# Attention and expert routing on one core: where a batch's gating stands in the turns of the attention loop

## The chip, the cores and the metric

The kernel runs on one core of one Trainium2 chip. The metric is the device time of one execution in microseconds (us); lower is better. Before the change the median of three runs is 442.36 us (441.19, 442.36 and 442.59).

The engines in the rows: PE is TensorE's matmuls, PEld its weight loads, DVE is VectorE, ACT is ScalarE, POOL is GpSimd, SP is SyncE, which here issues most of the DMAs. Each engine works through its own instructions in the order in which they were written for it, and waits where an operand or a buffer isn't there yet.

## The reference, cut to what matters

Blocked causal attention for 8 batches of 8 heads, 576 tokens of 64 values each, with blocks of 64; its output, 4608 tokens of 512 values, goes into a mixture of 8 experts in which each token has one expert and each expert keeps the 80 tokens with the largest gate weight:

```python
scores = where(block_i >= block_j, q @ k.T / 8, -1e9)
attn = exp(scores - scores.max(-1)); attn /= attn.sum(-1)
x = (attn @ v)                       # [4608, 512]
logits = x @ w_gate                  # [4608, 8]
expert_idx = argmax(logits, 1)
gate_w = softmax(logits)[expert_idx]
for e in range(8):
    tok = the (at most) 80 tokens of expert e with the largest gate_w
    out[tok] = gate_w[tok] * (relu(x[tok] @ w1[e]) @ w2[e])   # all other rows 0
```

The gating is the part from logits to gate_w. The change concerns how and when it is done, batch by batch, while the attention of later batches goes on.

## The kernel before, in words

The attention works on 32 pairs of heads, four pairs to a batch. One pass of the loop `for i in range(-3, n + 2)` is called a turn here. The tuple TURN at the top of the file is a turn written out by hand: a list of operations, each with an offset that says which pair it belongs to. It fixes the order of the instructions on every engine. For one pair the operations are:

- `prep` (L409, DVE transpose, and L412, POOL) lays out q and k.
- `scores` (L427, with a mask product at L434) makes the scores of query rows in three groups, "3", "20" and "1"; `scores_4` (L443) makes those of the last 64 rows of both heads. Their results lie in PSUM tiles named sc, of which there are two. So "1" takes over the tile of "3", and `scores_4` that of "20".
- `max` (L448) and `max_4` (L452) take row maxima on DVE; `soft` (L456) and `soft_4` (L461) take the exponentials on ACT, each with a second instruction that reads the row sum.
- `back` (L492, and L475 for its small part "44") transposes the exponentials on PE in 64-row halves, in parts C, A and B. C needs `soft_4` of the turn before. `take` copies results out of PSUM, on ACT (L532) or DVE (L534).
- `values` 0 and 1 (L522) multiply by v; `flip` (L275) transposes the result on DVE for the store.

The PSUM tiles of `back`, `values` and the gating come from one pool of four, named pm.

Within a turn PE's order is: scores 3, back C, scores 20, [first step], back 44, values 0, scores 1, back A, values 1, scores_4, back B, [second step], [third step]. The three entries "step" of TURN each take one entry from a list `todo` and run it. DVE's order around them is: max 3, max 20, [first step], prep 1, max 1, copy of A, flip, max_4, copy of B, [second step], [third step], prep 0 of the next turn, max 3 of the next turn. ACT's is: copies of C, soft 3 twice, [first step], soft 0, soft 2, copy of 44, soft 2, soft 0, copy of values 0, soft 1 twice, copy of values 1, copy of A, [second step], soft_4, copy of B, [third step].

When a batch's four pairs are done, nine gating steps are put on `todo`: `recip` (L268 to L271, reciprocals of the row sums, DVE), `store` (six DMAs on SP), `logits` for the first 384 tokens and then for the other 192 (L292 on PE with a copy on ACT at L294), `logits2` for four token tiles and then for the fifth (L304 transposes on PE with all 128 rows, products with the reciprocals on DVE at L310, a sum over heads at L319), `gate` (nine DVE instructions from L327 to L341, and one exponential on ACT at L330), `turn` (L349, POOL) and `turn2` (L358, the placing product on PE, and its copy to Wt on DVE, L362). Three go into each of three turns; in every fourth turn the list is empty. The last batch's gating comes after the loop, written out in order, and there `logits2` is split at three tiles.

After the attention the candidates of each expert are ranked, the 80 tokens of each are gathered, and the two expert products run while weights are loaded.

Of the kernel before, what the change touches and what calls it, by code (L numbers as in the profile page):

```python
# [7 lines left out]
F32 = mybir.dt.float32  # L8
# [5 lines left out]
ALU = mybir.AluOpType  # L14
AX = mybir.AxisListType
# [3 lines left out]
P = 128  # L19
BLK = 64  # L20
NT = 5
# [57 lines left out]
def tile_attn_moe(ctx, tc, q, k, v, w_gate, w1, w2, capacity, out, xs=None, dbg=None):  # L79
    nc = tc.nc  # L80
    B, H, S, D = q.shape
    NTOK, DM = out.shape
    E, _, F = w1.shape
    NP = H // 2
# [7 lines left out]
    def tok0(t):  # L92
        return P * t

    def tokn(t):
        return BLK if t == NT - 1 else P
# [62 lines left out]
    prod = sm1.tile([P, NT, H, E], F32, name="prod")  # L159

# [22 lines left out]
    def constants():  # L183
# [7 lines left out]
        nc.gpsimd.memset(prod[:, NT - 1], 0.0)  # L191
# [64 lines left out]
    class Batch:  # L256
# [28 lines left out]
        def logits(self, half):  # L285

            q0, q1 = ((0, 384), (384, 576))[half]
            if half == 0:
                self.lgT = sm.tile([P, S], F32, name="lgT", bufs=1)
            lt = ps_m.tile([P, 512], F32, name="pm")  # L290
            for pr in range(NP):
                nc.tensor.matmul(lt[32 * pr:32 * pr + 32, 0:q1 - q0], lhsT=wgd[:, pr, :],  # L292
                                 rhs=self.xT[:, pr, q0:q1], start=True, stop=True, tile_position=(0, 32 * pr))
            nc.scalar.copy(self.lgT[:, q0:q1], lt[:, 0:q1 - q0])  # L294

        def logits2(self, half, ends=(4, NT)):
            la = ps_m.tile([P, 512], F32, name="pm")
            rs = self.rs
            if half == 0:
                self.lg = sm.tile([P, NT, E], F32, name="lg", bufs=2)  # L300
            t0, t1 = (0, *ends)[half:half + 2]
            for t in range(t0, t1):
                n = tokn(t)
                self.turned = nc.tensor.transpose(la[0:n, P * (t - t0):P * (t - t0 + 1)],  # L304
                                                  self.lgT[:, tok0(t):tok0(t) + n], ident)
            for u0, u1, n in ((t0, min(t1, NT - 1), P), (NT - 1, t1, BLK)):
                if u0 < u1:
                    nu = u1 - u0
                    iv = la[0:n, P * (u0 - t0):P * (u1 - t0)].rearrange("p (r c) -> p r c", r=nu * NP)[:, :, 0:2 * E]
                    nc.vector.tensor_tensor(  # L310
                        prod[0:n, u0:u1].rearrange("p t (r s) e -> p (t r) s e", s=2),
                        iv.rearrange("p r (s e) -> p r s e", s=2),
                        rs[0:n, u0:u1].rearrange("p t (r s) -> p (t r) s", s=2).unsqueeze(3)
                        .broadcast_to([n, nu * NP, 2, E]), op=ALU.mult)
            if half == 0 and ends[0] == NT - 1:
                return
            if ends[0] == NT - 1:
                t0 = 0
            nc.vector.tensor_reduce(self.lg[:, t0:t1], prod[:, t0:t1].rearrange("p t h e -> p t e h"), axis=AX.X,  # L319
                                    op=ALU.add)  # L320
# [238 lines left out]
    def step():  # L559
        if todo:  # L560
            f, *args = todo.pop(0)
            f(*args)

    with tc.manual_schedule():
        warm(WARM[0], ps_m.tile([P, 512], F32, name="pm"))
        for i in range(-3, n + 2):
# [22 lines left out]
            if i >= 2 and (i - 2) % NP == NP - 1 and i - 2 < n - 1:  # L589
                bt = batches[(i - 2) // NP]  # L590
                todo += [(bt.recip,), (bt.store,), (bt.logits, 0), (bt.logits, 1), (bt.logits2, 0), (bt.logits2, 1), (bt.gate,),
                         (bt.turn, nc.gpsimd)] + [(bt.turn2,)]
# [8 lines left out]
        bt.logits(0)  # L601
        bt.logits(1)
        bt.logits2(0, (3, NT))
        bt.logits2(1, (3, NT))
# [504 lines left out]
```

## Time and profile before

| | us |
|---|---|
| median of three runs | 442.36 |
| the profiled execution's own time | 441.93 |
| its span (first to last instruction) | 440.2 |

So 1.73 us of the profiled execution lie outside its span. In a timeline row the first number is the start from the beginning of the span, the second the time from the first start to the last end of the instructions that the row merges; then engine, line, operation, result and operands, shapes and the count. A bracket gives how long the engine sat idle before the row and what ended that. A matmul of two fp32 operands shows as two records. PE pulls weight loads ahead, and matmuls overlap, so the distance between two starts is what a step costs PE, not the duration in its row.

### The profile page before, as it was taken

The page shows a single profiled execution, that of the slowest core. Times are in us where ns is not written, and L with a number is a line of the kernel's source. Part 1 is how long each engine was busy: PE and PEld are TensorE (multiplying, and loading weights), DVE is VectorE, ACT ScalarE, POOL GpSimd, SP SyncE. Part 2 cuts the span into 40 slices and gives each one's busy share as a digit, 9 for nine tenths or more (in the row PEclk, how much of TensorE's full clock was granted, in tenths as well). Part 3 has the DMA queues.
Part 4 walks back from the last instruction along what each step waited for, and adds up shares of the span by engine and source line. Part 5 has one row for each costly group of instructions (what it writes and reads, how often), then busy time and mean ns, then how long its engine had stood idle before and what let it go on. Part 6 is the DMA issues. An engine that isn't in the chain of part 4 may idle for free. (4 is left out here: it accounts for less than half of the span.)

```text
span 440.2 us, 14257 instructions
## 1 busy us (share of the span) xinstructions
PE 409.2 (93%) x5755; PEld 263.4 (60%) x5755; DVE 280.1 (64%) x559; ACT 288.3 (65%) x887; POOL 65.9 (15%) x133
## 2 busy tenths in 40 slices
PE   5899999999999999999999999999868899999970
PEld 3466666666666566666666656666546855666510
DVE  5677788888798888879879887986682131100000
ACT  1698888798788879888887887888520123333230
POOL 5001111011111101112111010210026201100000
PEclk9899999999999999999999999999997899999996
DMA  9677878988786998898879887854087999999000
GB/s 130 117 133 165 174 125 212 241 171 165 190 164 130 158 291 171 167 210 178 170 136 281 167 173 192 179 128 110 2 224 245 324 405 410 412 401 357 20 15 21
DMA packets 230168, 84.34 MB, mean 192 GB/s; under 512 B 196877, under 2 KB 215309, under 8 KB 230096
## 3 DMA queue, kind: packets, MB, share of 16 engines
q1 hardware_dynamic: 222528, 64.91, 63.5%
q0 software_dynamic: 5200, 18.16, 11.9%
q8 instruction: 47, 0.77, 0.7%
q10 hardware_dynamic: 2368, 0.30, 0.6%
q14 instruction: 25, 0.20, 0.1%
HBM read 63.21 MB, written 20.33 MB: 190 GB/s over the span
## 5 line engine op out<-in xcount | busy, mean ns | idle before, releaser
L456 ACT ACTIVATE P<-sc,negm 128x128 f32<-128x128 f32 (+3 forms) x256 | 133.4, 531 | 16.2 <-DVE negm L448 14.5
L448 DVE TENSOR_REDUCE negm<-sc 128x2 f32<-128x1024 f32 (+3 forms) x128 | 100.6, 811 | 38.5 <-PE sc L434 38.4
L427 PE MATMUL sc<-T,T 64*128 64x128 f32 (+3 forms) x512 | 94.6, 468 | 2.2 <-POOL T L412 1.3
L492 PEld LDWEIGHTS pm<-ident,P 64*128 64x128 f32 x1536 | 56.4, 139 | 33.1 <-ACT xT L532 11.0
L492 PE MATMUL pm<-ident,P 64*128 64x64 f32 x1536 | 68.8, 229 | 1.9 <-DVE prod L310 0.4
L522 PE MATMUL pm<-PT,vn 128*64 128x128 f32 (+1 forms) x512 | 60.7, 379 | 0.0
L427 PEld LDWEIGHTS sc<-T,T 64*128 64x128 f32 x512 | 42.6, 191 | 23.7 <-issue 7.2
L412 POOL TENSOR_SCALAR T<-T 128x576 f32<-128x576 f32 x32 | 21.4, 668 | 227.0 <-DVE T L409 227.0
L456 ACT ACTIVATION_READ_ACCUMULATOR P<-sc,negm 128x1 f32 x256 | 52.6, 205 | 0.0
L409 DVE STREAM_TRANSPOSE T<-ld 128x576 f32<-128x576 f32 x64 | 48.7, 763 | 1.4 <-DMA ld<-in_q_dram 1.4
L522 PE MATMUL pm<-PF,vn 128*64 128x64 f32 (+1 forms) x768 | 48.2, 247 | 0.9 <-ACT PF L532 0.9
L522 PEld LDWEIGHTS pm<-PT,vn 128*64 128x64 f32 x512 | 33.5, 137 | 22.9 <-issue 22.9
L884 PE MATMUL av<-w,hT 128*32 128x512 f32 (+1 forms) x320 | 43.1, 594 | 1.6 <-DVE y L889 1.6
L532 ACT COPY PF<-pm 128x512 f32<-128x512 f32 x64 | 34.4, 588 | 15.0 <-PE pm L492 15.0
L843 PE MATMUL ps<-xsT,w 128*64 128x80 f32 x1024 | 40.7, 239 | 3.7 <-issue 3.7
L534 DVE COPY PT<-pm 128x512 f32<-128x512 f32 x64 | 43.5, 680 | 0.3 <-PE pm L492 0.3
L843 PEld LDWEIGHTS ps<-xsT,w 128*64 128x64 f32 x1024 | 38.3, 141 | 7.5 <-issue 7.0
L889 DVE SCALAR_TENSOR_TENSOR y<-av,comb,yt 80x512 f32<-80x512 f32 x8 | 6.0, 746 | 57.2 <-ACT yt L887 51.0
L443 PE MATMUL sc<-T,T 64*64 64x288 f32 x256 | 39.0, 424 | 1.2 <-ACT P L456 1.2
L461 ACT ACTIVATE P<-sc,negm 128x576 f32<-128x576 f32 x32 | 23.7, 741 | 22.1 <-DVE negm L452 22.1
L532 ACT COPY PT<-pm 128x512 f32<-128x512 f32 x64 | 37.8, 591 | 0.0
L522 PEld LDWEIGHTS pm<-PF,vn 128*64 128x64 f32 x768 | 32.0, 137 | 7.4 <-ACT PF L532 1.1
(168 smaller groups left out, 419.2 us busy)
## 6 DMA issues: line engine op xcount, KB each, us to landing
w<-in_moe_w_dram SPq DMA_DIRECT2D x13, 2048.0 KB, 19.2
ld<-in_q_dram SPq DMA_DIRECT2D x128, 72.0 KB, 3.2
out_dram<-zero POOLq DMA_DIRECT2D x18, 512.0 KB, 3.8
xs<-Y SPq DMA_DIRECT2D x32, 288.0 KB, 4.9
ld<-in_k_dram SPq DMA_DIRECT2D x124, 72.0 KB, 2.8
vn<-in_v_dram SPq DMA_DIRECT2D x64, 128.0 KB, 3.0
w<-in_moe_w_dram POOLq DMA_DIRECT2D x3, 2048.0 KB, 11.1
vt<-in_v_dram SPq DMA_DIRECT2D x32, 32.0 KB, 2.9
```

Source lines behind the costliest of these rows:

```text
L409: nc.vector.transpose(t, self.nat[x].rearrange("p g d -> p (g d)"))
L427: nc.tensor.matmul(s[:, h, c:c + P * (u + 1)], lhsT=self.T[0][r, P * u:P * (u + 1)], rhs=self.T[1][r, 0:P * (u + 1)], start=(x == 0), stop ...
L443: nc.tensor.matmul(s[r, c, 0:288], lhsT=self.T[0][r, 512:S], rhs=self.T[1][r, 288 * c:288 * (c + 1)], start=True, stop=True)
L448: nc.vector.tensor_reduce(self.negm[:, u], self.s[g][:, :, c:c + P * (u + 1)], axis=AX.X, op=ALU.max, negate=True)
L456: nc.scalar.activation(Pt[self.i % 2][u][:, h], self.s[g][:, h, c:c + P * (u + 1)], AF.Exp, bias=self.negm[:, u, h:h + 1], scale=1.0, accu ...
L461: nc.scalar.activation(Pt[self.i % 2][4][:, 0:S].rearrange("p (c k) -> p c k", c=2), self.s["4"][:, :, 0:288], AF.Exp, bias=self.negm[:, 4 ...
L492: nc.tensor.transpose(pt[c][:, n_ * BLK:(n_ + 1) * BLK], from_[r, P * j:P * (j + 1)], ident[r, r])
L522: nc.tensor.matmul(to, lhsT=lhs, rhs=rhs, start=(n_ == 0), stop=(n_ == len(steps) - 1))
L532: nc.scalar.copy(*self.out.pop((what, x)))
L534: nc.vector.tensor_copy(*self.out.pop((what, x)))
L843: yield nc.tensor.matmul(dst(b)[64 * c:64 * (c + 1)], lhsT=w_[:, a, col:col + 64], rhs=x_[:, a], start=(a == 0), stop=(a == n - 1))
L884: last = nc.tensor.matmul(to[col:col + s1 - s0], lhsT=hT[:, a, s0:s1], rhs=w_[:, a], start=(a == ends[0]), stop=(a == ends[1]), tile_posit ...
```

## The change

`logits` makes both products, of 384 and of 192 tokens, in one step, each with its own pm tile and copy. Its result lgT becomes one tile of 640 columns whose last 64 are zeroed once at the start (before, the product tile's last part was zeroed). `logits2` is one step: five token tiles are transposed in the two halves of 64 rows, ten transposes of 64 rows each into two pm tiles, then four products on DVE (one for each pair of heads, over all five token tiles) and one sum. An entry of `todo` may be None, which leaves a step empty. The list of a batch is now ten long: in its first turn logits, recip, store; in the second logits2, nothing, gate; in the third nothing, turn, nothing; in the fourth turn2.

```diff
+    lgT = sm1.tile([P, NT * P], F32, name="lgT")
...
-        nc.gpsimd.memset(prod[:, NT - 1], 0.0)
+        nc.gpsimd.memset(lgT[:, S:], 0.0)
...
+        def logits(self):
+
+            for q0, q1 in ((0, 384), (384, S)):
+                lt = ps_m.tile([P, 512], F32, name="pm")
+                for pr in range(NP):
+                    nc.tensor.matmul(lt[32 * pr:32 * pr + 32, 0:q1 - q0], lhsT=wgd[:, pr, :],
+                                     rhs=self.xT[:, pr, q0:q1], start=True, stop=True, tile_position=(0, 32 * pr))
+                nc.scalar.copy(lgT[:, q0:q1], lt[:, 0:q1 - q0])
+
+        def logits2(self):
+            la = [ps_m.tile([P, 512], F32, name="pm") for _ in range(2)]
+            self.lg = sm.tile([P, NT, E], F32, name="lg", bufs=2)
+            for t in range(NT):
+                for c in range(2):
+                    r = slice(c * BLK, (c + 1) * BLK)
+                    self.turned = nc.tensor.transpose(la[c][:, BLK * t:BLK * (t + 1)], lgT[r, P * t:P * (t + 1)],
+                                                      ident[r, r])
             for pr in range(NP):
...
+                iv = la[pr // 2][:, 0:BLK * NT].rearrange("p (t r c) -> p t r c", t=NT, r=2)[:, :, pr % 2, 0:2 * E]
+                nc.vector.tensor_tensor(
+                    prod[:, :, 2 * pr:2 * pr + 2], iv.rearrange("p t (s e) -> p t s e", s=2),
+                    self.rs[:, :, 2 * pr:2 * pr + 2].unsqueeze(3).broadcast_to([P, NT, 2, E]), op=ALU.mult)
+            nc.vector.tensor_reduce(self.lg, prod.rearrange("p t h e -> p t e h"), axis=AX.X, op=ALU.add)
...
     def step():
-        if todo:
-            f, *args = todo.pop(0)
-            f(*args)
+        x = todo.pop(0) if todo else None
+        if x:
+            x[0](*x[1:])
...
-                todo += [(bt.recip,), (bt.store,), (bt.logits, 0), (bt.logits, 1), (bt.logits2, 0), (bt.logits2, 1), (bt.gate,),
-                         (bt.turn, nc.gpsimd)] + [(bt.turn2,)]
+                todo += [(bt.logits,), (bt.recip,), (bt.store,), (bt.logits2,), None, (bt.gate,),
+                         None, (bt.turn, nc.gpsimd), None, (bt.turn2,)]
...
-        bt.logits(0)
-        bt.logits(1)
-        bt.logits2(0, (3, NT))
-        bt.logits2(1, (3, NT))
+        bt.logits()
+        bt.logits2()
```

## Rows read from the trace of the kernel before

**Rows 1.** The page: busy time of each engine and its share of the span.

```profile
PE 409.2 (93%) x5755; PEld 263.4 (60%) x5755; DVE 280.1 (64%) x559; ACT 288.3 (65%) x887; POOL 65.9 (15%) x133
```

**Rows 2.** Single turns, each from one start of scores 3 to the next: the stretch and its length, then busy time (and instructions) of PE, PEld, DVE, ACT and POOL, the granted clock of TensorE, the DMA share and GB/s. First a turn without gating, ahead of the first batch's gating; then the second, third and fourth turn of the first batch's gating; then the first turn of the second batch's.

```profile
54.49:63.50 9.01, 8.87 (x129) 5.74 (x127) 7.09 (x11) 7.84 (x25) 0.66 (x1) 1.00 0.69 124
73.40:83.38 9.98, 9.98 (x141) 6.52 (x137) 7.12 (x11) 8.27 (x28) 1.53 (x3) 1.00 0.99 298
83.38:92.61 9.23, 9.23 (x140) 6.15 (x139) 8.99 (x22) 7.68 (x26) 2.00 (x3) 1.00 0.81 150
92.61:101.38 8.77, 8.77 (x132) 5.80 (x125) 6.96 (x12) 7.84 (x25) 0.66 (x1) 1.00 0.90 153
101.38:111.28 9.90, 9.76 (x138) 5.94 (x134) 8.75 (x17) 8.37 (x26) 1.26 (x2) 1.00 0.81 175
```

**Rows 3.** The timeline of PE in the turn without gating: scores 3, back C, scores 1, scores_4 and back B (the next scores 3 starts at 63.50).

```profile
54.49 1.08 PE L427 MATMUL sc<-T,T 64*128 64x512 f32 x4
...
55.73 0.71 PE L492 MATMUL pm<-ident,P 64*128 64x64 f32 x16
...
59.92 0.70 PE L427 MATMUL sc<-T,T 64*128 64x256 f32 x4
...
61.84 1.19 PE L443 MATMUL sc<-T,T 64*64 64x288 f32 x8
62.95 0.72 PE L492 MATMUL pm<-ident,P 64*128 64x64 f32 x16
```

**Rows 4.** The timelines of ACT (soft_4 of the turn before, the two soft 3, then this turn's soft_4) and of DVE (max 3, and max 1 with the wait ahead of it) over the same turn.

```profile
54.85 0.74 ACT L461 ACTIVATE P<-sc,negm 128x576 f32<-128x576 f32 x1 [0.78 <-DVE negm L452]
...
57.44 0.70 ACT L456 ACTIVATE P<-sc,negm 128x512 f32<-128x512 f32 x1
...
58.11 0.70 ACT L456 ACTIVATE P<-sc,negm 128x512 f32<-128x512 f32 x1
...
63.87 0.74 ACT L461 ACTIVATE P<-sc,negm 128x576 f32<-128x576 f32 x1 [0.78 <-DVE negm L452]
...
56.02 1.18 DVE L448 TENSOR_REDUCE negm<-sc 128x2 f32<-128x1024 f32 x1
...
60.69 0.69 DVE L448 TENSOR_REDUCE negm<-sc 128x2 f32<-128x512 f32 x1 [1.25 <-PE sc L434]
```

**Rows 5.** The timeline of PE where gating stands: the product of 192 tokens and back 44 behind it; the five full transposes (scores 3 follows at 83.38) and back C of that turn; turn2 (scores 3 follows at 92.61); the product of 384 tokens (scores 3 follows at 111.28).

```profile
75.99 0.53 PE L292 MATMUL pm<-xT,wgd 128*32 128x192 f32 x8
76.45 0.30 PE L475 MATMUL pm<-ident,P 128*64 128x128 f32 x1
...
82.68 0.77 PE L304 MATMUL pm<-ident,lgT 128*128 128x128 f32 x5
...
84.37 0.70 PE L492 MATMUL pm<-ident,P 64*128 64x64 f32 x16
...
92.33 0.35 PE L358 MATMUL pm<-sp,sameR 128*32 128x40 f32 x16
...
110.49 0.85 PE L292 MATMUL pm<-xT,wgd 128*32 128x384 f32 x8
```

**Rows 6.** The weight loads of `back`: the page's group (busy us and mean ns of one), and the sixteen of one back B in the timeline of the weight loads.

```profile
L492 PEld LDWEIGHTS pm<-ident,P 64*128 64x128 f32 x1536 | 56.4, 139 | 33.1 <-ACT xT L532 11.0
...
53.94 0.57 PEld L492 LDWEIGHTS pm<-ident,P 64*128 64x128 f32 x16 [0.44 <-ACT xT L532]
```

**Rows 7.** The timeline of DVE around the start of the turn at 83.38: the two products and the sum of logits2, prep 0, max 3 with max 20; the first of the nine instructions of gate and prep 1 behind the last; and, a turn and a half later, the first of recip and prep 1 behind it. At the end soft 3 on ACT in the turn at 83.38.

```profile
83.43 0.54 DVE L310 TENSOR_TENSOR prod<-pm,rs 128x256 f32<-128x256 f32 x2
84.00 0.74 DVE L319 TENSOR_REDUCE lg<-prod 128x40 f32<-128x320 f32 x1
84.66 0.77 DVE L409 STREAM_TRANSPOSE T<-ld 128x576 f32<-128x576 f32 x1
85.35 2.38 DVE L448 TENSOR_REDUCE negm<-sc 128x2 f32<-128x1024 f32 x3
87.65 0.18 DVE L327 TENSOR_REDUCE mx<-lg 128x5 f32<-128x40 f32 x1
...
89.42 0.78 DVE L409 STREAM_TRANSPOSE T<-ld 128x576 f32<-128x576 f32 x1
...
105.56 0.33 DVE L269 COPY sums<-sums 64x4 f32<-64x4 f32 x2
...
106.47 0.72 DVE L409 STREAM_TRANSPOSE T<-ld 128x576 f32<-128x576 f32 x1
...
86.65 0.69 ACT L456 ACTIVATE P<-sc,negm 128x512 f32<-128x512 f32 x1 [0.49 <-DVE negm L448]
```

**Rows 8.** The timeline of the first turn of all: the second soft 3 on ACT and scores 1 on PE.

```profile
12.40 0.68 ACT L456 ACTIVATE P<-sc,negm 128x512 f32<-128x512 f32 x1
...
13.22 0.70 PE L427 MATMUL sc<-T,T 64*128 64x256 f32 x4 [0.97 <-ACT P L456]
```

**Rows 9.** The end of the attention: scores 3 and scores_4 of the last pair on PE, and the first of the products of the last batch's logits2 and the first row of its gate on DVE.

```profile
300.70 1.13 PE L427 MATMUL sc<-T,T 64*128 64x512 f32 x4
...
308.22 1.19 PE L443 MATMUL sc<-T,T 64*64 64x288 f32 x8
...
318.20 0.36 DVE L310 TENSOR_TENSOR prod<-pm,rs 128x192 f32<-128x192 f32 x1
...
319.87 0.20 DVE L327 TENSOR_REDUCE mx<-lg 128x5 f32<-128x40 f32 x1
```

More of the change, by code (lines that the diff above doesn't have):

```diff
@@ L283, in store @@
                                                 self.Y[32 * i:32 * i + 32].rearrange("r j a c -> r j (a c)"))
[L285 to L290, printed above, removed]
-            for pr in range(NP):
-                nc.tensor.matmul(lt[32 * pr:32 * pr + 32, 0:q1 - q0], lhsT=wgd[:, pr, :],
-                                 rhs=self.xT[:, pr, q0:q1], start=True, stop=True, tile_position=(0, 32 * pr))
-            nc.scalar.copy(self.lgT[:, q0:q1], lt[:, 0:q1 - q0])
@@ L296, in logits2 @@
[L296 to L320, printed above, removed]
```

## The prediction

> **What bounds the kernel now.** The page comes first: PE is busy 93% of the span, DVE and ACT 64% and 65% [rows 1], so PE sets the pace unless something makes it wait. An average can't tell where, so the next view is the table of single turns. [...] Four turns make up a batch. The four from 73.40 to 111.28, with every gating step in them once, take 9.98 + 9.23 + 8.77 + 9.90 = 37.88 us, and one of them is shorter than the turn without gating: 8.77 [rows 2]. That is what the reader is to look at: gating work makes the turn behind it cheaper.
>
> The timelines say why. Without gating, back C starts 1.24 us after scores 3 (54.49 to 55.73) [rows 3]; where the full transposes stand ahead of scores 3 it is 0.99 (83.38 to 84.37) [rows 2, 5]. The 0.25 is a wait: back C needs soft_4, which starts at 54.85 and is followed by back C 0.88 later [rows 3, 4], and soft_4 starts 2.03 after scores_4 (61.84 to 63.87) [rows 3, 4], by way of max_4. Between scores_4 and back C PE has only back B and scores 3 to do, so 0.25 us are left open. In three turns of four the kernel before fills them, with the product of 384 tokens, the transposes, or turn2, all of which PE does between back B and scores 3 [rows 5].
>
> **The change part by part, per batch.** All of PE's gating work moves to the first step, between scores 20 and back 44. So none lies between back B and scores 3, and each of the four turns starts from the 9.01 of the turn without gating. The cover is gone; the 0.25 comes back in three turns, about 0.75 us.
>
> First turn, logits: the product of 384 tokens costs 0.79 us (110.49 to 111.28), that of 192 costs 0.46 (75.99 to 76.45) [rows 2, 5]; same instructions, so 9.01 + 1.25 = 10.26. The two copies of lgT move ahead of soft 0 on ACT, which PE's own 1.25 gives time for. recip now follows the copy of B on DVE and pushes max 3 of the second turn by 0.91 (105.56 to 106.47) [rows 7]. The six DMAs of store keep their place on SP, as no DMA stands between the two steps; they wait some 1 us more for recip, and behind them wait loads of q and k that are used two turns later.
>
> Second turn, logits2: ten transposes of 64 rows instead of five of 128. The full ones cost 0.70 (82.68 to 83.38) [rows 2, 5]. The shape of the halves is that of back B: sixteen in 0.55 (62.95 to 63.50) [rows 2, 3], 0.034 each, so ten cost 0.34; the upper bound is that ten cost what the five did. I take 0.34, from the row of the same shape: 9.01 + 0.34 = 9.35.
> [...] One load here does take 139 ns, but the sixteen of a back B fit in 0.57 us together [rows 6], since the two halves load beside each other and beside matmuls; so the trace decides for 0.34.
>
> On DVE two products and a sum (83.43 to 84.66: 1.23) become four products and a sum. Two products took 0.57 and the sum 0.66 [rows 7]; four, each of 80 elements in place of 256 and 64, lie between 0.57 and 1.14, and I take 0.8, near the sizes. They wait for the transposes, with prep 1 and max 1 queued behind. The load on DVE in this turn is 0.91 + 0.8 + 0.66 = 2.4; it has 1.25 idle ahead of max 1 alone [rows 4], 7.09 busy of 9.01 in all [rows 2], so 1.92, and 0.34 more from PE's shift, 2.3. This just fits: cost between 0 (all hidden) and 0.45 (four products at 1.14), taken as 0.
>
> gate, at the end of the second turn, is the large term. Its nine instructions hold DVE for 1.77 us (87.65 to 89.42) [rows 7]. Before, they stood behind max 20, where nothing on PE waits soon. Now they stand between the copy of B and prep 0, and max 3 is behind them. max 3 starts 1.53 into a turn (54.49 to 56.02) [rows 3, 4]; now 1.53 + 1.77 = 3.30. soft 3 follows max 3 by 1.30 (85.35 to 86.65) [rows 7], so at 4.60 instead of 2.95 (54.49 to 57.44) [rows 3, 4]. The second soft 3 is 0.67 behind (57.44 to 58.11) [rows 4], and scores 1, which needs the PSUM tile that the soft 3 read, starts 0.82 after the second one, as the first turn of all shows, where PE waited 0.97 for it [rows 8]: 4.60 + 0.67 + 0.82 = 6.09 instead of 5.43 (54.49 to 59.92) [rows 3]. PE waits 0.66 us; with 0.04 for the tile of scores_4, which needs the ACT instructions behind, I take 0.70. Bounds: the third turn of before, which carries 1.23 of products and sum at the same spot, costs 9.23 - 0.28 for turn2 = 8.95, 0.18 over the 8.77 [rows 2, 5, 7]; that is the lower end. The upper end is that all of ACT's delay of 1.65 less its idle 0.78 ahead of soft_4 [rows 4] reaches the next back C: 0.87. Third turn: 9.01 + 0.70 = 9.71.
> [...]
>
> Fourth turn: turn2 costs 0.28 (92.33 to 92.61) [rows 2, 5]: 9.29. turn itself on POOL has two turns' time.
>
> Sum of a batch: 10.26 + 9.35 + 9.71 + 9.29 = 38.61, against 37.88: 0.73 us more. Six whole batches make 4.38. The seventh pays 10.26 - 9.90 = 0.36 in its first turn; in its second, scores_4 came 7.52 after scores 3 (300.70 to 308.22) [rows 9] and now comes 7.35 (54.49 to 61.84) [rows 3] + 0.34 = 7.69 after it, 0.17 more; from scores_4 on the end hangs on soft_4 as before. In the last batch products and sums took 1.67 (318.20 to 319.87) [rows 9]; four products and a sum take 1.37 to 1.80: taken as no change. Together 4.38 + 0.36 + 0.17 = 4.91. The experts' part starts later by as much. Profiled execution: 441.93 + 4.91 = 446.8; the median of the runs is 0.43 above the profiled one, so 442.36 + 4.91 = 447.3 us. With both open terms at their ends (gate 0.18 to 0.87, DVE 0 to 0.45) a batch is 0.21 to 1.35 over, and my own range is 444.1 to 451.0.
>
> **The rivals.** *PE's own work decides* (faster): with waits filled by other work, a batch's gating falls on PE from 0.79 + 0.46 + 0.70 + 0.28 = 2.23 to 1.87; seven times 0.36 is 2.5, 439.8 us. It decides if soft_4 is done before scores 3 ends and soft 3 before scores 1. For it: PE is busy 93% and the turns with gating leave it no idle time [rows 1, 2]. Against it: the 0.25 in turns without gating [rows 3].
>
> *gate is hidden* (no change): scores 1 doesn't wait, since the score tile that it takes is another. Then a batch is 38.61 - 0.70 = 37.91, and the end pays 0.53: 443.1 us. Against it: the first turn shows the wait [rows 8].
>
> *DVE overflows in the second turn*: recip, four products and sum exceed the slack by 0.45, max_4 and soft_4 come late, and gate's 1.77 is pushed as well: 0.73 + 0.45 + 0.17 a batch, 442.36 + 6 x 1.35 + 0.53 = 451.0 us. For it: the sum above fits by nothing.
>
> *The half loads don't overlap*: ten loads at 139 ns one after the other take 1.39 instead of 0.34 [rows 6], 7.4 us in seven batches: 454.6. [...]
>
> **How the numbers follow.** Forecast 0.68, PE alone 0.10, gate hidden 0.12, DVE overflow 0.08, loads 0.02. A measurement of this kernel can tell about 0.3% from no change, 441.0 to 443.7. So faster 0.10, same 0.12, slower 0.78. The range reaches from the hidden gate, 442.6, to 450.3, short of the overflow and the rival below; that leaves out 0.2.
>
> **What would show it.** Right: scores 3 to back C at about 1.24 in all four turns; turns of about 10.3, 9.4, 9.7 and 9.3; in the third an idle PE ahead of scores 1, put down to ACT's soft 3, and soft 3 waiting some 1.6 us for max 3; ten transposes within 0.4. Wrong: a third turn of 9.0 (gate hidden), turns near 8.8 (the cover not lost), a wait of max_4 on DVE in the second turn (overflow).

## The result, and the profile after

The changed kernel takes 445.85 us (median of 7 runs, 443.92 to 446.76), the kernel before on the same chip 441.88 (7 runs, 441.19 to 443.64). The ratio is 1.0092 with a 95% interval of 1.0074 to 1.0109: 3.97 us slower. The forecast was 4.91 us slower. The changed kernel's profiled execution takes 446.24 us, its span 444.0, so 3.8 us of span have to be found; the profile and the timelines below are of it. Outside the span lie 2.24 us, where it was 1.73 before. (The profiled executions of two experiments, e2_turn2_end and e12_four_ends, are slow ones with one turn of 16 to 17 us each, so only their other turns are used.)

The page of the kernel after, busy time of each engine, beside [rows 1]:

```profile
PE 406.6 (92%) x5795; PEld 260.5 (59%) x5795; DVE 280.3 (63%) x573; ACT 286.6 (65%) x887; POOL 65.4 (15%) x133
```

PE has 2.6 us less to do and the kernel is 3.8 us longer. What is added is not work, so a view that shows waits is needed. The table of turns comes first, as [rows 2]: a turn without gating, then the four turns of the first batch's gating (columns as there).

```profile
54.80:63.82 9.02, 8.88 (x130) 5.75 (x127) 7.10 (x11) 7.84 (x25) 0.66 (x1) 1.00 0.72 133
63.82:73.92 10.10, 9.96 (x146) 6.16 (x143) 7.09 (x11) 8.36 (x27) 1.20 (x2) 1.00 0.63 135
73.92:83.22 9.30, 9.16 (x140) 6.13 (x137) 8.98 (x20) 7.81 (x25) 1.53 (x3) 1.00 0.48 148
83.22:93.02 9.80, 9.01 (x130) 5.79 (x127) 8.62 (x20) 7.67 (x26) 1.97 (x3) 1.00 1.11 292
93.02:102.27 9.25, 9.13 (x145) 5.97 (x143) 7.29 (x12) 8.06 (x26) 0.66 (x1) 1.00 0.69 122
```

The batch takes 10.10 + 9.30 + 9.80 + 9.25 = 38.45 us against 37.88 [rows 2], 0.57 more, and the other five repeat it within 0.02, but for one of 38.61. In the third turn PE is busy only 9.01 of 9.80; in the others its idle time is 0.12 to 0.14. The granted clock is 1.00 in all of them.

The span adds up: 0.32 ahead of the first batch's gating (63.82 against 63.50), 3.61 in six batches, 0.20 in the first turn of the seventh (10.10 against 9.90), and about 0.3 less from there to the end: 3.8.

The timeline of PE over the second and third turn shows where the idle time is: scores 3, back C, logits2 with back 44 behind it, scores 3 and back C of the third turn, its scores 1 and scores_4.

```profile
73.92 1.08 PE L415 MATMUL sc<-T,T 64*128 64x512 f32 x4
...
75.16 0.71 PE L480 MATMUL pm<-ident,P 64*128 64x64 f32 x16
...
76.69 0.47 PE L301 MATMUL pm<-ident,lgT 64*128 64x64 f32 x10
77.09 0.30 PE L463 MATMUL pm<-ident,P 128*64 128x128 f32 x1
...
83.22 1.08 PE L415 MATMUL sc<-T,T 64*128 64x512 f32 x4
...
84.47 0.71 PE L480 MATMUL pm<-ident,P 64*128 64x64 f32 x16
...
89.37 0.70 PE L415 MATMUL sc<-T,T 64*128 64x256 f32 x4 [0.65 <-ACT P L444]
...
91.33 1.19 PE L431 MATMUL sc<-T,T 64*64 64x288 f32 x8
```

Scores 3 to back C is 1.24 and 1.25 (73.92 to 75.16, 83.22 to 84.47), the value of the turn without gating [rows 3]: nothing fills the wait for soft_4 any more. The ten half transposes hold PE for 0.40 (76.69 to 77.09). And ahead of scores 1 PE waits 0.65 for soft 3 (P at L444). DVE and ACT around that wait, in two fences: on DVE the end of the second turn and gate with what is behind it, on ACT the soft 3 that PE waits for.

```profile
82.79 0.76 DVE L440 TENSOR_REDUCE negm<-sc 128x1 f32<-128x576 f32 x1 [0.21 <-PE sc L431]
83.46 0.68 DVE L522 COPY PT<-pm 128x512 f32<-128x512 f32 x1
84.06 0.18 DVE L315 TENSOR_REDUCE mx<-lg 128x5 f32<-128x40 f32 x1
...
85.86 0.78 DVE L397 STREAM_TRANSPOSE T<-ld 128x576 f32<-128x576 f32 x1
86.57 2.38 DVE L436 TENSOR_REDUCE negm<-sc 128x2 f32<-128x1024 f32 x3
```

```profile
87.87 0.69 ACT L444 ACTIVATE P<-sc,negm 128x512 f32<-128x512 f32 x1 [1.59 <-DVE negm L436]
```

gate holds DVE from 84.06 to 85.86, prep 0 and max 3 queue behind it, soft 3 waits 1.59 for max 3, PE waits 0.65 for soft 3. In none of these turns is DVE the engine with the most to do, and still it is the one that is late. The first row carries a second reading: the only idle time that DVE has between the max_4 of the first turn and that of the second is 0.21, ahead of this max_4. recip, four products and the sum fit into the second turn by that much.

### The profile page after: what moved, and what is told of

Read it like the earlier page. It is cut to its first block, busy times and chain, and to the rows that moved or that the text cites. A ratio compares the mean times of both kernels' runs of the same rounds, so it can differ in the third digit from the quotient of the medians.

```text
span 444.0 us, 14346 instructions
## 1 busy us (share of the span) xinstructions
PE 406.6 (92%) x5795; PEld 260.5 (59%) x5795; DVE 280.3 (63%) x573; ACT 286.6 (65%) x887; POOL 65.4 (15%) x133
## 5 line engine op out<-in xcount | busy, mean ns | idle before, releaser
L444 ACT ACTIVATE P<-sc,negm 128x128 f32<-128x128 f32 (+3 forms) x256 | 133.3, 532 | 30.3 <-DVE negm L436 29.8
L436 DVE TENSOR_REDUCE negm<-sc 128x2 f32<-128x1024 f32 (+3 forms) x128 | 99.5, 807 | 37.0 <-PE sc L422 37.0
L444 ACT ACTIVATION_READ_ACCUMULATOR P<-sc,negm 128x1 f32 x256 | 53.1, 207 | 0.0
```

The costliest lines, as they stand in the source:

```text
L436: nc.vector.tensor_reduce(self.negm[:, u], self.s[g][:, :, c:c + P * (u + 1)], axis=AX.X, op=ALU.max, negate=True)
L444: nc.scalar.activation(Pt[self.i % 2][u][:, h], self.s[g][:, h, c:c + P * (u + 1)], AF.Exp, bias=self.negm[:, u, h:h + 1], scale=1.0, accu ...
```

## The experiments

Each turn is taken from one start of scores 3 to the next; a batch is four turns. The row gives the first batch, and the other batches repeat it within 0.04, but for single fourth turns that come under "recip and SP". In e4 and e12 the first turn of the first batch takes 9.89, since no gating stands ahead of it yet, and the row gives the second batch. The ratio is to the kernel before on the same chip; e1 to e4, e5 to e8 and e9 to e12 ran on one chip each.

| version | turns of a batch, us | batch | ratio, 95% interval |
|---|---|---|---|
| before (e9_before_again) | 9.89 9.98 9.25 8.77 | 37.89 | 1.0008, 0.9987 to 1.0029 |
| after, first measurement | 10.10 9.30 9.80 9.25 | 38.45 | 1.0092, 1.0074 to 1.0109 |
| after (e5_after_again) | 10.11 9.31 9.79 9.27 | 38.48 | 1.0137, 1.0107 to 1.0167 |
| e1_gate_mid | 10.10 9.30 9.02 9.27 | 37.69 | 1.0082, 1.0053 to 1.0111 |
| e2_turn2_end | 10.10 9.30 10.18 8.73 | 38.31 | 1.0115, 1.0070 to 1.0160 |
| e3_dummy_end | 10.10 9.30 9.80 9.26 | 38.46 | 1.0112, 1.0073 to 1.0152 |
| e4_before_gate_end | 9.61 9.98 8.74 10.16 | 38.49 | 1.0193, 1.0150 to 1.0236 |
| e6_recip_first | 10.10 9.31 9.80 9.25 | 38.46 | 1.0097, 1.0069 to 1.0125 |
| e7_recip_first_gate_mid | 10.10 9.31 9.01 9.28 | 37.70 | 1.0046, 1.0018 to 1.0073 |
| e8_before_recip_late | 9.89 9.98 9.24 8.77 | 37.88 | 1.0048, 1.0014 to 1.0082 |
| e10_places_of_before | 10.22 9.05 9.86 8.76 | 37.89 | 1.0038, 1.0019 to 1.0057 |
| e11_logits_end | 10.22 9.04 9.80 9.27 | 38.33 | 1.0116, 1.0085 to 1.0147 |
| e12_four_ends | 9.65 9.30 9.05 9.85 | 37.85 | 1.0048, 1.0012 to 1.0084 |

Two things have to be kept in mind with the ratios. Every version but the kernel before has 2.04 to 2.24 us of each run outside the span, the kernel before 1.68 to 1.86; so some 0.3 to 0.4 us of each difference lie outside the loop, in e4 and e8 too, which differ from the kernel before in the order of the steps alone. The cause wasn't looked into. And the intervals of e1, e2, e3, e6 and e11 overlap both of the changed kernel's, so what these five show, they show in their turns and not in their times.

### Where gate stands

The changed kernel with gate one step later, in the first step of the third turn, behind max 20:

```diff
-                todo += [(bt.logits,), (bt.recip,), (bt.store,), (bt.logits2,), None, (bt.gate,),
-                         None, (bt.turn, nc.gpsimd), None, (bt.turn2,)]
+                todo += [(bt.logits,), (bt.recip,), (bt.store,), (bt.logits2,), None, None,
+                         (bt.gate,), (bt.turn, nc.gpsimd), None, (bt.turn2,)]
```

> The changed kernel with one edit: gate goes from the third step of a batch's second turn to the first step of its third turn, behind max 20 on DVE, where it stood before the change. Theory (gate's place holds max 3, soft 3 and so scores 1): the idle PE of 0.65 us ahead of scores 1 in the third turn is gone, that turn takes 9.0 to 9.1 us instead of 9.80, a batch about 37.7 instead of 38.45, and the time falls by about 4.7 us to some 441. Rival (the lost cover ahead of back C, or two PSUM tiles taken at once, make up the loss): the third turn keeps its length and the time stays near 446.

The third turn falls from 9.80 to 9.02, the length of a turn without gating, and the other turns of the batch stay. So gate's place costs 0.78 a batch, and without it the changed batch is 0.20 shorter than the batch before. The time that was expected, 4.7 us less than the changed kernel's, was missed: the ratio is 1.0082 against 1.0092 and 1.0137. Two of e1's fourth turns are 0.94 and 1.50 longer, so of six times 0.78 its attention keeps 2.3 us (238.73 from the first batch's gating to the last scores 3, against 241.01); what makes them longer comes under "recip and SP". The other way round, the kernel before with gate moved to the end of a turn (an entry of todo may be None there, as in the change):

```diff
-                todo += [(bt.recip,), (bt.store,), (bt.logits, 0), (bt.logits, 1), (bt.logits2, 0), (bt.logits2, 1), (bt.gate,),
-                         (bt.turn, nc.gpsimd)] + [(bt.turn2,)]
+                todo += [(bt.recip,), (bt.store,), (bt.logits, 0), (bt.logits, 1), (bt.logits2, 0), (bt.logits2, 1),
+                         None, None, (bt.gate,), (bt.turn, nc.gpsimd), (bt.turn2,)]
```

> The kernel before the change with gate, turn and turn2 put later: gate in the third step of a batch's third turn (behind the copy of B on DVE, ahead of the next max 3), turn and turn2 in the first and second step of its fourth turn. Theory of gate's place: PE waits 0.6 to 0.7 us ahead of scores 1 in the fourth turn; the four turns of a batch take about 9.98, 8.85, 10.0 and 9.65, together 38.5 instead of 37.88, and the time rises by 4 to 5 us to about 446.5. Rival (gate costs the same wherever DVE does it): about 442, no more than the end of the last batch's turn later.

The batch grows from 37.89 to 38.49, with none of the other parts of the change. So the move costs this kernel too, 0.60 a batch; turn2, which had to move along, now fills the cover of the next batch's first turn (9.61 against 9.89) and takes a part back. (The time is 8.1 us longer, 446.49 against 438.43, though six batches explain only 3.6; in its profile 3.2 more than in e9 lie behind the last scores 3, see the last section. That it is the 446.5 of the expectation is luck, since the kernel before is 3.9 us faster on this chip than the 442.36 that the expectation started from.)

### The lost cover

Three versions put PE's gating work back ahead of scores 3, or something in its place. turn2 in the last step of the third turn:

```diff
-                         None, (bt.turn, nc.gpsimd), None, (bt.turn2,)]
+                         None, (bt.turn, nc.gpsimd), (bt.turn2,)]
```

> The changed kernel with one edit: turn2 goes from the first step of a batch's fourth turn to the third step of its third turn, between back B and the next scores 3 on PE. Theory of the cover (0.25 us of PE's work at that spot costs nothing, since PE waits there for soft_4 anyway): scores 3 to back C falls from 1.24 to 0.99 in the fourth turn, third and fourth turn together take 18.80 instead of 19.05, and the time falls by 1.5 to 1.8 us to about 444.2. Rival (only the amount of PE's work counts): no change.

Both products in the last step of the first turn, with recip and store early again:

```diff
-                todo += [(bt.logits,), (bt.recip,), (bt.store,), (bt.logits2,), None, (bt.gate,),
+                todo += [(bt.recip,), (bt.store,), (bt.logits,), (bt.logits2,), None, (bt.gate,),
```

> The changed kernel with one thing moved: recip and store come first and second and both products third in the first turn; all else as changed. Theory of the lost cover: the first turn stays 10.1 (9.0 + 1.1), the second falls from 9.30 to 9.05, with scores 3 to back C about 1.0 instead of 1.24; third 9.8, fourth 9.25; 38.2 a batch, 1.5 us faster than the changed kernel, and SP's late loads of q are gone with the early store. Rival (the place of PE's work does not matter): 38.45 a batch, the time of the changed kernel.

And three useless half transposes behind back B in every turn:

```diff
+            if 0 <= i < n:
+                idle = ps_m.tile([P, 512], F32, name="pm")
+                for x in range(3):
+                    nc.tensor.transpose(idle[:, x * BLK:(x + 1) * BLK], ident[0:BLK, :], ident[0:BLK, 0:BLK])
```

> The changed kernel with work added: at the end of each of the 32 turns with a pair, behind back B, PE makes three transposes of 64 rows of the identity into a PSUM tile that nobody reads, about 0.2 us. Theory of the cover: they lie in the wait of 0.25 us ahead of back C and cost under 0.05 us a turn, so the time rises by less than 1.6 us. Rival (PE's work sets the time): 32 times 0.2, 6.4 us more, 452.

The last is the plainest: no turn became longer by the added work, so there is a hole of at least that size. By count that is some 0.1 us, three of sixteen that take 0.55 [rows 2, 3], not the 0.2 of the expectation. Its PE timeline, with the transposes of L578 around the next scores 3 and back C behind:

```profile
80.97 0.72 PE L480 MATMUL pm<-ident,P 64*128 64x64 f32 x16
81.51 0.29 PE L578 MATMUL pm<-ident 64*128 64x64 f32 x2
81.58 0.69 PE L415 MATMUL sc<-T,T 64*128 64x512 f32 x1
81.64 0.23 PE L578 MATMUL pm<-ident 64*128 64x64 f32 x1
81.70 1.07 PE L415 MATMUL sc<-T,T 64*128 64x512 f32 x3
...
82.76 0.71 PE L480 MATMUL pm<-ident,P 64*128 64x64 f32 x16
```

From back B to back C it is 1.79 us (80.97 to 82.76); in the changed kernel 1.80 (82.67 to 84.47). What was added only shortened the wait.

In the two others the turn behind the moved piece is shorter by 0.26 (9.30 to 9.04) and by about 0.52 (9.25 to 8.73, of which 0.24 is turn2 itself, so 0.28 is cover). But the turn that now carries the piece at its end grew by more than in the middle: both products cost 10.22 - 9.01 = 1.21 there and 1.09 in the first step, turn2 0.38 and 0.24. The PE timeline of e11_logits_end says where most of this comes from:

```profile
70.59 0.72 PE L480 MATMUL pm<-ident,P 64*128 64x64 f32 x16
71.23 1.18 PE L291 MATMUL pm<-xT,wgd 128*32 128x384 f32 x16
72.34 1.13 PE L415 MATMUL sc<-T,T 64*128 64x512 f32 x4
73.33 0.69 PE L480 MATMUL pm<-ident,P 64*128 64x64 f32 x16
```

back C comes 0.99 behind scores 3 (72.34 to 73.33), so the cover works, and the product takes the same 1.11 as in the first step. But back B ahead of it holds PE for 0.64 (70.59 to 71.23) where ahead of scores 3 it holds it for 0.55 [rows 2, 3]. So a covered turn gains about 0.25 gross and 0.13 to 0.15 net. Both versions missed their expectation of the full 0.25, and neither's time is lower than the changed kernel's by more than its spread.

### recip and SP

Three versions ask what recip's later place does. e6 takes recip into the first step beside the products and the store into the second; e7 is that with gate as in e1; e8 delays recip and store by one step in the kernel before.

```diff
-                todo += [(bt.logits,), (bt.recip,), (bt.store,), (bt.logits2,), None, (bt.gate,),
+                todo += [(lambda bt=bt: (bt.recip(), bt.logits()),), (bt.store,), None, (bt.logits2,), None, (bt.gate,),
```

```diff
-                todo += [(bt.recip,), (bt.store,), (bt.logits, 0), (bt.logits, 1), (bt.logits2, 0), (bt.logits2, 1), (bt.gate,),
-                         (bt.turn, nc.gpsimd)] + [(bt.turn2,)]
+                todo += [None, (bt.recip,), (lambda bt=bt: (bt.store(), bt.logits(0)),), (bt.logits, 1), (bt.logits2, 0),
+                         (bt.logits2, 1), (bt.gate,), (bt.turn, nc.gpsimd), (bt.turn2,)]
```

> The changed kernel as it is, for comparison on the same chip as the three others of this set. Both theories: 3.5 to 4.5 us above the kernel before; turns of a batch 10.10, 9.30, 9.80 and 9.25; SP stands about 7 us ahead of the first batch's store, waiting for recip.

> The changed kernel with recip put back into the first step of a batch's first turn, together with logits, and store into the second step. Theory of a second loss (SP waits a turn for recip ahead of the store, the loads of q and k behind it come late, and DVE's prep waits for them in the turns after the large weight loads): SP's 27 us of waiting for recip shrink to under 2 us but for the last batch's, prep waits for no load after the start, the turns keep 10.10, 9.30, 9.80 and 9.25, and the time is 0.3 to 2 us below the changed kernel's and spreads less. Rival (the loads had slack enough): the same time as the changed kernel within 0.3 us.

> As the run with recip first, and with gate in the first step of the third turn in addition. Theory (gate's place and recip's place are what loses; the joined product and the half transposes gain): turns of 10.10, 9.30, 9.02 and 9.25, a batch 37.67 against 37.88 before, no wait of prep for loads, so 1 to 1.5 us faster than the kernel before, about 5.5 us faster than the changed one. Rival (something else of the change costs time too): still 2 us or more slower than the kernel before.

> The kernel before with recip alone moved one step back, to where the changed kernel has it: first step empty, recip in the second, store and the first product in the third; all else as before. Theory of the late loads: SP waits 5 to 8 us for recip in the first batch, prep waits for loads of q here and there, and the time is 0.5 to 3 us above the kernel before. max 3 of the next turn is 0.9 us later too, but PE's product of 384 tokens covers most of that: under 0.3 us a batch. Rival: the same time as before within 0.3%.

recip's place changes no turn: e6 has the turns of e5, and e8 those of before. DVE has room for it in either turn. (The ratio of e6 is lower than that of e5, but their intervals overlap, and their attention takes 240.90 and 240.91 us, so in the attention e6's rival holds: no turn is longer for the late recip there. e5 lies 5.3 us above the kernel before, more than expected. e8 is slower than before, as expected, but its interval doesn't exclude the 0.3% of its rival.) What it changes is SP. In the kernel before the first store follows the loads of v at once; the changed kernel's SP timeline has a hole:

```profile
67.55 1.40 SPq L392 DMA_DIRECT2D vt<-in_v_dram  x1
75.77 0.38 SPq L280 DMA_DIRECT2D xs<-rs  x1
76.20 1.64 SPq L281 DMA_DIRECT2D xs<-rs  x1
...
83.66 6.44 SPq L382 DMA_DIRECT2D ld<-in_q_dram  x4
```

and the same place before:

```profile
67.95 0.61 SPq L404 DMA_DIRECT2D vt<-in_v_dram  x1
68.70 0.49 SPq L279 DMA_DIRECT2D xs<-rs  x1
69.25 0.60 SPq L280 DMA_DIRECT2D xs<-rs  x1
...
73.36 4.98 SPq L394 DMA_DIRECT2D ld<-in_q_dram  x4
```

SP stands for 6.8 us (68.95 to 75.77) where it hardly stood, because it reaches the store most of a turn before DVE reaches recip's new place: recip's last instruction ends at 75.74, before the change at 68.67. (In e5 SP stands 5.1 us, in e8 5.9.) The loads of q behind the store start 10.3 us later (83.66 against 73.36). The table of waits shows DVE waiting for loads of q: what waits for what, us in total, times, the longest. First after, then before measured again (e9_before_again).

```profile
DVE T L397 <- DMA ld<-in_q_dram: 3.8, 4, 1.3
```

```profile
DVE T L409 <- DMA ld<-in_q_dram: 1.5, 2, 0.9
```

Two waits in each, of 0.5 to 0.9, lie at the start. The other two of the changed kernel are of 1.33 and 1.05, in the fourth turns of the third and the fifth batch, and all that it loses by them is 0.13 in the first of these turns. The other versions say why: the turn becomes longer only by what exceeds some 1.2 us of wait. e1 waits 2.16 and 2.71 there and loses 0.94 and 1.50 (turns of 10.21 and 10.77), e7 waits 2.35 and loses 1.13. With the turns of before there is less room, 0.8: e8 waits 1.66 and loses 0.84 (9.61). The DVE row of e7:

```profile
246.21 0.78 DVE L397 STREAM_TRANSPOSE T<-ld 128x576 f32<-128x576 f32 x1 [2.35 <-DMA ld<-in_q_dram]
```

That SP's hole is the cause of these waits isn't shown. SP stands for recip in the first, the seventh and the last batch alone (27.0 us in three waits); in the second to the sixth it comes to the store after recip is done, and the late loads are in the third and fifth. In all five profiles with the late recip, e2's left out, DVE waits for loads of q after the start (after, e1, e3, e5, e8); of the seven with the early one, e12's left out, two have such a wait too (e7, e10). e10, with the store early, waits 2.04 in the fourth turn of the fifth batch and loses 1.21. What makes SP late there wasn't settled.

So e7, which by its turns should save 6 x 0.19 = 1.1 us, loses 1.13 in that one turn and 0.20 in the first turn of the seventh batch. Its attention takes 237.44 us from the first batch's gating to the last scores 3, against 237.22 in e9, and its time is 1.0046 (1.0018 to 1.0073) of the time before. Its theory was missed. By the medians it is 2.0 us slower, the least that its rival named; 0.2 of that lie in the attention and 0.3 to 0.4 outside the span, and where the rest lies isn't settled, so the rival stands open.

### The cheap parts in the old places

If the parts are cheaper and only their places cost, then the changed parts in the places of the kernel before should win:

```diff
-                todo += [(bt.logits,), (bt.recip,), (bt.store,), (bt.logits2,), None, (bt.gate,),
-                         None, (bt.turn, nc.gpsimd), None, (bt.turn2,)]
+                todo += [(bt.recip,), (bt.store,), (bt.logits,), None, None, (bt.logits2,),
+                         (bt.gate,), (bt.turn, nc.gpsimd), (bt.turn2,)]
```

> The kernel before, unchanged, so that its trace and that of the versions beside it come from one chip: turns of 9.9, 10.0, 9.2 and 8.8 us, 37.9 a batch; time within 0.3% of the kernel before.

> The change's joined products and half transposes, but the gating steps in the places of the kernel before: recip, store and both products in the first turn (products last), logits2 last in the second, gate, turn and turn2 in the third, nothing in the fourth. Theory (the parts are cheaper, the places cost): three turns of four start with PE's work ahead of scores 3 and so lose no 0.25; gate stands behind max 20; store is issued early. Turns of 10.1, 9.2, 9.3 and 8.8 = 37.4 a batch against 37.9 before and 38.45 changed: 3 us faster than before, some 6 faster than the changed kernel. Rival (the parts themselves cost, by DVE's four products or by the half transposes): 38 or more a batch, no faster than before.

37.89 a batch, that of before; neither the theory (37.4) nor the time it gave. The third turn is 9.86, not 9.3. Its table of turns, third and fourth turn:

```profile
83.22:93.08 9.86, 9.59 (x146) 6.24 (x142) 9.62 (x26) 8.11 (x26) 2.00 (x3) 1.00 0.81 162
93.08:101.84 8.76, 8.76 (x131) 5.80 (x125) 6.94 (x12) 7.83 (x25) 0.66 (x1) 1.00 0.85 155
```

DVE is busy 9.62 of 9.86 in the turn that has both the products of logits2 and gate. Its timeline, from max_4 of the second turn to max_4 of the third, has no bracket between:

```profile
82.48 0.76 DVE L440 TENSOR_REDUCE negm<-sc 128x1 f32<-128x576 f32 x1 [0.41 <-PE sc L431]
83.16 0.68 DVE L522 COPY PT<-pm 128x512 f32<-128x512 f32 x1
83.75 0.67 DVE L305 TENSOR_TENSOR prod<-pm,rs 128x80 f32<-128x80 f32 x4
84.46 0.74 DVE L308 TENSOR_REDUCE lg<-prod 128x40 f32<-128x320 f32 x1
85.11 0.77 DVE L397 STREAM_TRANSPOSE T<-ld 128x576 f32<-128x576 f32 x1
85.80 2.39 DVE L436 TENSOR_REDUCE negm<-sc 128x2 f32<-128x1024 f32 x3
88.11 0.18 DVE L315 TENSOR_REDUCE mx<-lg 128x5 f32<-128x40 f32 x1
...
92.44 0.72 DVE L440 TENSOR_REDUCE negm<-sc 128x1 f32<-128x576 f32 x1
```

82.48 to 92.44 is 9.96 us of DVE without a gap. So this stretch is bound by DVE. The kernel before has the same stretch, in part in [rows 7], from max_4 to max_4 without a gap between:

```profile
82.16 0.76 DVE L452 TENSOR_REDUCE negm<-sc 128x1 f32<-128x576 f32 x1 [0.41 <-PE sc L443]
...
91.98 0.72 DVE L452 TENSOR_REDUCE negm<-sc 128x1 f32<-128x576 f32 x1
```

There it takes 9.82 us; products and sum take 0.13 less (1.23 against 1.36). Up to the first of these max_4 e10 is 0.13 shorter than before, counted from the start of the batch (18.53 against 18.66), the stretch is 0.14 longer, and from its end to the end of the batch both take 9.40. So what the half transposes save PE within the stretch (0.31 us from 82.91 to the scores 3 at 83.22, against 0.70 for the full ones [rows 2, 5]) is worth nothing: PE is idle for 0.27 of the third turn, where before it had no idle time [rows 2]. The rival named DVE's four products, and its "no faster than before" came true; that DVE binds this stretch before the change as well was in neither. The last version, with a piece of PE's work at the end of all four turns, runs into the same wall (the list of the first six batches; logits takes its parts as arguments there):

```diff
+                    todo += [(bt.recip,), (bt.store,), (bt.logits, 0), None, None, (bt.logits, 1), None, None, (bt.logits2,),
+                             (bt.gate,), (bt.turn, nc.gpsimd), (bt.turn2,)]
```

> The changed parts, but each of a batch's four turns ends in a piece of PE's gating work ahead of the next scores 3: the product of 384 in the first, that of 192 in the second, logits2 in the third, turn2 in the fourth (gate and turn ahead of it there); for the seventh batch the list of e10_places_of_before. Theory: all four turns fill the 0.25; turns of 9.5, 9.2, 9.2 and 9.3 = 37.2 a batch, 1 us faster than e10_places_of_before, 4 faster than before. Rival: the two products apart cost 0.14 more than together, and DVE's work behind logits2 takes the rest: no faster than e10_places_of_before.

Its last turn, in which DVE has the products and gate, is 9.85, and from max_4 to max_4 DVE again takes 9.96 without a gap (127.71 to 137.67). The second and third are short (9.30 and 9.05), the first is 9.65 where 9.5 was expected, and the batch ends at 37.85: the theory (37.2) was missed, and the rival's "no faster than e10" came true. No version ran faster than the kernel before. The shortest batch, 37.69 in e1 and 37.70 in e7, is the one that has logits2 and gate a full turn apart, both in a first step; their times are still above those of before.

## Why the prediction was right

**The mechanism.** gate's nine instructions ahead of max 3 were the large term: 0.70 predicted, 0.78 by e1 against the changed kernel (9.80 to 9.02). The chain stood as it was told: max 3, soft 3 (1.59 us of wait against "some 1.6"), scores 1 (0.65 of wait against 0.66, and 6.15 after scores 3 against 6.09). The 0.04 for the tile of scores_4 had no row; the trace has it (91.33 - 89.37 = 1.96 against 1.92 [rows 3]). The rival that gate is hidden falls with the 0.65 and with e1 and e4; the one that PE's own work decides falls with the distance from scores 3 to back C, 1.22 to 1.25 in every turn from the first gating on.

**The first turn** was mis-sized: 1.25 for both products, read from one piece at the end of a turn and one in a first step; together in the first step they cost 1.09 (10.10 against 9.01), 0.16 less in every batch, the largest error of the sum. The errors of the other turns (0.05 and 0.04 too high, 0.09 too low) cancel. e11 shows that most of it lies in the place: 0.12 more at the end, of which 0.09 is back B's.

**The second turn**: the ten half transposes hold PE for 0.40 against 0.34, but the turn is 9.30 against 9.35, since the mask product ahead of them (L422) holds PE 0.09 less than in a turn without gating (0.06 against 0.15). The rival that half loads don't overlap (1.39) falls: the ten loads, of 139 ns each, take 0.39 us together. Products and sum took 1.35 (78.61 to 79.96), within the bounds and 0.11 under the value taken.

```profile
78.61 0.67 DVE L305 TENSOR_TENSOR prod<-pm,rs 128x80 f32<-128x80 f32 x4
79.31 0.73 DVE L308 TENSOR_REDUCE lg<-prod 128x40 f32<-128x320 f32 x1
79.96 0.77 DVE L397 STREAM_TRANSPOSE T<-ld 128x576 f32<-128x576 f32 x1
```

"This just fits" stood on a load of 2.4 against a room of 2.3, which by its own numbers is 0.1 too much; it held, with 0.21 of idle time left ahead of max_4. The rival that DVE overflows didn't come true here; e10 and e12 are what it looks like.

**The cover** was right in kind and told too simply. 0.25 a turn is what is lost gross; the products (e11) and turn2 (e2) became cheaper by 0.12 and 0.14 by leaving the end of the turn. For the transposes, which changed in kind too, it isn't shown; if it holds for them, about half of the 0.75 was returned. The prediction's sum took this in only where it had a row of the new place (192 tokens), which is the main reason why it lies above the measurement.

**Sum.** 0.57 a batch against 0.73: 3.61 in six batches against 4.38; 0.20 against 0.36 in the seventh's first turn; behind it about 0.3 less against 0.17 more, 0.32 ahead of the first gating and 0.5 outside the span against nothing. The first two of these parts nearly cancel, which is luck: the last section shows that such parts move without any change. Of the 0.17 the trace has 0.12 (scores_4 of the last pair 7.64 after scores 3). The range is stated twice, 444.1 to 451.0 and 442.6 to 450.3; the lower end of the second is called the hidden gate, whose own sum is 443.1. The measurement lies in both. For the last batch's products and sums the lower bound of 1.37 follows from no row (0.57 + 0.66 = 1.23).

**The step that failed without costing** is SP's: "some 1 us more for recip" was 6.8 us of standing. recip moves by a step of the list, and on DVE that is 7 us (68.67 to 75.74), while SP is at the store at the same time as before. The term stood at nothing in the time, and in the changed kernel the waits for loads cost 0.13. In e1 and e8, with recip as late, they cost 2.44 and 0.84, but whether by way of this hole isn't shown.

## What to carry to other kernels

DVE, busy 63% of the span, set the pace of the third turn all the same (PE waited 0.65 us there): look at what is queued behind a moved block on its engine, and who waits for that, not at the engine's busy share. Before placing two blocks on the same engine, read the stretch between two of its fixed points (here max_4 to max_4) for gaps: beside the 9.96 us without one in e10_places_of_before, a saving of 0.39 us on PE was worth nothing, and PE was idle for 0.27 of the turn. SP's queue, which ran ahead of the engines in the first batch, stood there for 6.8 us when recip came 7 us later; look at when a queue's instruction is reached, not at its place in the turn. A gain of some tenths a turn is read from the turns: here it was shown there and didn't come out in the times.

## What the runs showed of the hardware

The kernel before, unchanged, reached the first batch's gating at 63.50 us in one profile and at 62.19 in the other (e9). The table of stretches for 14 to 21 us, first before, then e9, shows a lower granted clock in the one that came later:

```profile
14.00:21.00 7.00, 5.81 (x68) 3.48 (x66) 4.18 (x9) 4.90 (x18) 0.13 (x1) 0.76 0.80 142
```

```profile
14.00:21.00 7.00, 5.96 (x84) 3.66 (x81) 5.60 (x11) 5.86 (x19) 0.67 (x1) 1.00 0.80 144
```

In the first the granted clock was 0.50 from 16 to 18 us; scores_4, which starts at 15.67 there, takes 2.19 us where it takes 1.19 in e9. PE was idle in pieces ahead of it, while the loop filled, but by about as much in both (1.26, 0.97 and 1.19 us before, 1.34, 1.26 and 0.90 in e9), so what decided isn't shown. Nor does the granted clock of the traces go with every such row: e7 shows 1.00 over this stretch, though its scores_4 takes 2.19. The changed kernel has 0.76 there too in its first profile, so the two compared above are alike. In the second comparison, of two chips, e5 (0.53 there) starts its first gating at 63.67 and e9 at 62.19: 1.48 of the 5.6 us between their spans (442.0 and 436.4) come from there, 3.69 from the attention, as in the first comparison (3.81), and 0.43 from behind it. The part behind the last scores 3 took 135.9 to 140.2 us in these fourteen profiles, 139.5 and 137.0 in the two of before, by causes that weren't looked into. So differences of the attention, turn by turn, are settled to some hundredths, and the times of whole runs only to 1 or 2 us.

Back B's sixteen half transposes hold PE for 0.55 us where scores 3 comes next, and for 0.64 where the product of L291 (e11_logits_end) or the full transposes of the kernel before come next. The ten half transposes of logits2 hold it for 0.31 ahead of scores 3 (82.91 to 83.22 in e10_places_of_before) and for 0.40 ahead of back 44; the mask product of L422 for 0.06 ahead of the half transposes (76.63 to 76.69) and for 0.15 ahead of back 44 (57.52 to 57.67, both in the changed kernel). Each time the dearer case is the one in which the next piece takes all 128 rows behind a piece of 64, and it is dearer by 0.09. This fits the cheaper place of the gating's pieces: in the first step that change of rows stands ahead of back 44 anyway, at the end of a turn it is added. The profile gives no cause for it.
